# A recomputed hand-written order for a fused attention and gated-FFN kernel

## The chip, the cores and the metric

The kernel runs on one core of a Trainium2 chip. The metric is the device time of one execution in microseconds; before the change it is 292.96 us (median of 3 runs, 292.79 to 294.41). The profiled execution took 292.72 us, of which 290.2 us lie between its first and its last instruction. Times of instructions below are counted from that first instruction.

## The reference

```
B, H, S, Nb, D = 8, 8, 576, 16, 64
k_all, v_all = concat([beacon_k, k]), concat([beacon_v, v])     # 16 + 576 keys
scores = q @ k_all.T / sqrt(D), causal over the last 576 keys, beacons always seen
x = softmax(scores) @ v_all           # rearranged to [B*S, H*D] = [4608, 512]
out = ((x @ w1) * (x @ w2)) @ w3 @ w_out    # w1, w2: 512 x 1024; w3: 1024 x 1024; w_out: 1024 x 512
```

Inputs and output are float32; the kernel computes with float16 operands and float32 sums.

## The kernel before, in words

Everything is held on the chip. `w3 @ w_out` is folded once into `Wt` (1024 x 512), so that a block of 512 rows of `x` needs the two projections (`a`, `b`), a product and one output matmul. There are 8 batches of attention and 9 blocks of 512 rows (`mc`), and TensorE works on both kinds of work in turn.

What sets the order of the work is a string, `ORDER`, with some 1,190 entries. The loop in line 665 calls a small function for each entry, and each engine gets its instructions in exactly this order; an instruction whose operand isn't ready blocks all that stand behind it on its engine. The entries, with batch `b`, 128-row chunk `c`, PSUM bank `n` and evicting engine (`A` for ScalarE, ACT; `D` for VectorE, DVE):

- Loads. `lq b c`, `lk b c`, `lv b c` load a chunk of q, k or v (for batch 0, a pair of heads of q or k), `lkb`, `lvb` the beacons, `l3 r` a block of 128 rows of w3 (line 398), `lo a` two blocks of w_out (line 401), `l1 c`, `l2 c` a 256-column block of w1 or w2 (line 389). All are issued by GpSimd (POOL) on one software queue, in order, and a load waits for the landing of the one that had its semaphore before, eight loads earlier. Only `lq 0 0` and `lk 0 0` are issued by SyncE and ScalarE on queues of their own; these are the two first queues of the change's name.
- Folding. `t3 r n` transposes a w3 block on TensorE (line 481), `e3` evicts it, `f r a n` multiplies it by a quarter of w_out (line 491), four of them make a row block of `Wt`, and `ew` evicts that.
- Attention. `cast` and `tq`, `tk` (TensorE transposes) with `eq`, `ek` (evictions) bring q and k into place for batches 0 to 2; later batches (and `Dq 2 4`) use DMA transposes on SyncE (`Dq`, `Dk`). `s b g n` computes a group of score blocks (line 504; 13 groups `g` a batch, the two heads of a pair as matmuls on 64 rows each), `exp` is the activation on ACT (line 517), `m` masks the diagonal on DVE, `v b t h n` is the product with v (line 533) and `n` normalizes it on DVE (line 547; a reciprocal and a multiplication).
- `x` with `ex` transposes a chunk of the result on TensorE, `TX` by DMA instead (line 573). `a mc kf n` and `b mc kf n` are the projections (line 578; `a` with w1, `b` with w2, four matmuls of 512 columns), `ea` evicts the first to SBUF with a factor (ACT or DVE), `eb` multiplies the second by it (DVE only). `o mc mt n` is the output matmul (line 601), `eo` its eviction, `st` the store.
- `spin reps n` multiplies zeros (line 619) where TensorE would be idle at the start. `consts` are memsets and mask selections.

PSUM has one pair of banks for scores always (0), two pairs that are scores or single banks by turns (2 and 4), and two single banks (6, 7). There are three buffers for `ea` results (`asb`) and two of the transposed q, k, v and x. The casts of batch 0's q and k, `ea`, `eo`, `eq`, `ek`, `ex`, `e3` and `ew` name their engine in `ORDER`.

Of the kernel before, what the change touches and what calls it, by code (L numbers as in the profile page):

```python
# [190 lines left out]
def kernel(  # L191
# [427 lines left out]
    def spin(reps, n):  # L619
        for _ in range(reps):  # L620
            nc.tensor.matmul(bank(n), zeros[:, 0:P], zeros)
# [76 lines left out]
```

## Time and profile before

| engine | busy us of 290.2 | what it mostly does |
|---|---|---|
| TensorE, matmuls (PE) | 282.4 | projections, output, scores, PV, folding |
| ACT | 163.9 | 104 exp of 128 x 1024, evictions |
| DVE | 154.2 | `eb`, masks, normalizing, evictions |
| POOL | 133.5 | issues 26.19 MB of transfers on the software queue |

| load | us from issue to landing, median |
|---|---|
| w3 block | 6.1 |
| w_out blocks | 7.1 |
| w1, w2 block | 7.5 |
| 128-row chunk of q, k, v | 6.7 to 7.3 |
| first q, k on the SyncE and ACT queues | 4.2, 4.5 |

How to read this. The view of groups gives the busy time and the mean of one instruction of each kind; the view of waits gives, for each engine, whom it waited for. The landing of one load is its issue time in the timeline plus the time to landing that the DMA view gives for a stretch with this issue alone. Matmuls are pipelined, so the mean duration of one (379 ns for 512 columns) isn't its cost; the step from one start to the next is. The mean clock granted to TensorE was 1.000.

### The profile page before, as it was taken

How to read it: one execution, taken by the hardware profiler on the slowest of the kernel's cores; microseconds unless marked ns; L12 is line 12 of the kernel's file. 1: busy time of each engine (PE TensorE's matmuls, PEld its weight loads, DVE VectorE, ACT ScalarE, POOL GpSimd, SP SyncE). 2: the span in 40 equal slices, each digit the busy share in tenths (PEclk: the TensorE clock that was granted, in tenths of full speed). 3: DMA queues.
4: the chain of work that ended last, by engine and by line, in shares of the span. 5: the costliest groups of instructions: out<-in, count | busy, mean ns of one | idle time of the engine just before them, and what ended most of it. 6: DMA issues, size and time to landing. Idle time of an engine off the chain costs nothing.

```text
span 290.2 us, 7029 instructions
## 1 busy us (share of the span) xinstructions
PE 282.4 (97%) x2904; PEld 154.3 (53%) x2904; DVE 154.2 (53%) x344; ACT 163.9 (56%) x214; POOL 133.5 (46%) x186
## 2 busy tenths in 40 slices
PE   6999989999999999999999999999999999999995
PEld 2556655566565565565455544555465544444443
DVE  4338754786567677655456625534555653144500
ACT  3469655868684875386375527844475653232232
POOL 8579878996985452950956602930011001000000
PEclk9999999999999999999999999999999999999999
DMA  7999999999999999999999993999324014100033
GB/s 169 202 196 170 190 173 172 155 141 166 169 180 136 138 153 192 126 143 199 148 169 182 167 169 80 129 148 220 45 93 111 0 29 126 73 2 0 0 146 145
DMA packets 154319, 38.84 MB, mean 134 GB/s; under 512 B 144048, under 2 KB 149936, under 8 KB 154288
## 3 DMA queue, kind: packets, MB, share of 16 engines
q0 software_dynamic: 114720, 26.19, 99.2%
q1 hardware_dynamic: 39360, 11.92, 27.3%
q8 instruction: 22, 0.36, 0.5%
q10 hardware_dynamic: 208, 0.29, 0.3%
q14 instruction: 9, 0.07, 0.1%
HBM read 39.32 MB, written 9.44 MB: 168 GB/s over the span
## 4 chain that ended last, share of the span: by engine, by line
PE 84%; DMA 8%; POOL 5%; ACT 1%; issue 1%; DVE 0%; POOLq 0%
PE one L580 44%; PE one L601 21%; PE one L539 9%; PE pair L508 8%; DMA wo<-in_moe_w_out_dram 5%; DMA q<-in_q_dram 3%; PE one L428 1%; POOL va L340 1%; PE one L565 1%; POOL w L390 1%; POOL xT L399 1%; ACT ring L518 1%; POOL q L332 1%; POOL k L340 1%; POOL st L357 0%
## 5 line engine op out<-in xcount | busy, mean ns | idle before, releaser
L580 PE MATMUL one<-xT,w 128*128 128x512 f16 x576 | 133.0, 379 | 0.2 <-DVE xT L296 0.2
L518 ACT ACTIVATE ring<-pair 128x1024 f16<-128x1024 f32 x104 | 99.2, 1027 | 15.1 <-PE pair L508 14.8
L580 PEld LDWEIGHTS <-w 128*128 128x128 f16 x576 | 53.2, 98 | 59.9 <-issue 2.5
L595 DVE TENSOR_TENSOR gT<-one,asb 128x512 f16<-128x512 f32 x72 | 49.4, 690 | 55.1 <-PE one L580 41.3
L601 PE MATMUL one<-Wt,gT 128*128 128x512 f16 (+1 forms) x296 | 66.3, 373 | 0.0
L300 ACT ACTIVATE asb<-one 128x512 f32<-128x512 f32 x55 | 32.9, 599 | 58.7 <-PE one L580 37.1
L615 POOL DMA_DIRECT2D out_dram<-st x26 | 14.8, 569 | 69.9 <-DVE st L302 26.3
L601 PEld LDWEIGHTS <-gT 128*128 128x128 f16 x296 | 27.8, 98 | 30.2 <-issue 0.5
L340 POOL DMA_DIRECT2D va<-in_v_dram x40 | 34.0, 856 | 19.7 <-PE one L539 14.2
L539 PEld LDWEIGHTS <-ring 128*128 128x128 f16 x960 | 34.8, 97 | 10.2 <-issue 2.0
L539 PE MATMUL one<-va,ring 128*128 128x65 f16 x960 | 37.7, 193 | 0.5 <-DMA va<-in_v_dram 0.5
L300 ACT ACTIVATE st<-one 128x512 f32<-128x512 f32 (+1 forms) x26 | 15.1, 582 | 34.4 <-PE one L601 34.4
L551 DVE TENSOR_TENSOR x<-one,rd 128x384 f16<-128x384 f32 (+1 forms) x64 | 31.4, 491 | 2.2
L340 POOL DMA_DIRECT2D k<-in_k_dram x35 | 29.9, 860 | 4.5 <-issue 1.6
L332 POOL DMA_DIRECT2D q<-in_q_dram x35 | 30.2, 869 | 1.9 <-DMA q<-in_q_dram 0.9
L508 PE MATMUL pair<-qT,kT 64*128 64x80 f16 (+4 forms) x736 | 30.1, 225 | 0.1
L508 PEld LDWEIGHTS <-kT 64*128 64x128 f16 x736 | 19.9, 95 | 14.0 <-issue 10.2
L528 DVE TENSOR_TENSOR ring<-ring,MD 128x768 f16<-128x768 f16 x32 | 17.7, 553 | 10.2 <-ACT ring L518 10.2
L550 DVE RECIPROCAL rd<-one 128x6 f32<-128x6 f32 (+1 forms) x64 | 11.8, 185 | 20.7 <-PE one L539 20.5
L528 DVE TENSOR_TENSOR ring<-ring,MX 128x384 f16<-128x384 f16 x32 | 11.3, 352 | 10.1 <-ACT ring L518 9.9
L493 PE MATMUL one<-wo,gT 128*128 128x512 f16 x56 | 14.9, 380 | 0.4 <-DVE gT L296 0.3
L302 DVE TENSOR_SCALAR asb<-one 128x512 f32<-128x512 f32 x17 | 11.7, 689 | 3.5 <-PE one L580 3.5
(60 smaller groups left out, 126.8 us busy)
## 6 DMA issues: line engine op xcount, KB each, us to landing
out_dram<-st POOLq DMA_DIRECT2D x26, 256.0 KB, 6.2
...
```

What stands on the lines that cost most here:

```text
L300: nc.scalar.activation(dst, src, AF.Copy, scale=by)
L332: nc.gpsimd.dma_start(dst[:rows, c], src[b, :, ds(c * P, rows), :].rearrange("h s d -> s h d"))
L340: nc.gpsimd.dma_start(dst[ds(p0, rows), c], src[b, :, ds(s0, rows), :].rearrange("h s d -> s h d"))
L493: nc.tensor.matmul(bank(n), wT(r)[:, a, rt % 2, :], wo16[:, rt, :], start=(rt == 0), stop=(rt == NFT - 1),)
L508: nc.tensor.matmul(shape(n, "pair")[:, hh, ds(col, w)], kT[ds(hh * 64, 64), t, ts(jt, P)], qT[ds(hh * 64, 64), t, ds(q0, w)],)
L518: nc.scalar.activation(held(b, g)[:, :, 0:GW], shape(n, "pair"), AF.Exp, scale=scale)
L528: nc.vector.tensor_tensor(blk, blk, msk, ALU.mult)
L539: nc.tensor.matmul(pv[:, 2 * at + hh, 0 : D + 1], held(b, g)[:, hh, ds(col, P)], va[:, jt, 2 * t + hh, 0 : D + 1], start=(jt == 0), stop=( ...
L551: nc.vector.tensor_tensor(x16s[b % NB2][:, ds(2 * h, ni), ts(t, P)].rearrange("p i (h d) -> p i h d", h=2), pv[:, 0 : 2 * ni, 0:D].rearran ...
L580: nc.tensor.matmul(bank(n), w12[:, kt, ds(i * DF + kf * P, P)], xT[:, kt, ds(mc * 512, 512)], start=(kt == 0), stop=(kt == NKT - 1),)
L595: nc.vector.tensor_tensor(gTs[mc % 2][:, kf, :], bank(n), asb[slot["asb", (mc, kf)]], ALU.mult)
L601: nc.tensor.matmul(bank(n)[:, 0:w], gTs[mc % 2][:, kf, ts(mt, P)], Wt[:, kf, ds(c0, w)], start=(kf == 0), stop=(kf == NFT - 1),)
```

## The change

It gives a new `ORDER`, from the first entry to the last, recomputed for the landings of the two first queues, with the evicting engines (`A` or `D`) chosen by the same search. Loads of k and of the beacons now stand between the first w3 and w_out blocks. `TX 4 4` becomes `x 4 4 6` with `ex 4 4 D 6`. The last block to be finished is block 8, row tile 2, in place of block 7, row tile 0. Counts of engines, before and after: `ea` 55 A, 17 D and 33 A, 39 D; `eo` 26 A, 11 D and 15 A, 22 D; `e3` 8 D and 5 A, 3 D; `cast` 6 A, 2 D and 2 A, 6 D; `eq` 4 A, 9 D and 7 A, 6 D. The functions are as before but for one, which lets a spin write to the score pair:

```
 def spin(reps, n):
     for _ in range(reps):
-        nc.tensor.matmul(bank(n), zeros[:, 0:P], zeros)
+        nc.tensor.matmul(bank(n) if n else tiles[0][:, 0, :], zeros[:, 0:P], zeros)
```

The two orders up to the scores of batch 2 (the rest, some 85 lines on either side, is left out):

```
-consts 0; lq 0 0 S; lk 0 0 A; l3 2; consts 1; spin 8 7; l3 4; l3 3; lo 0; lkb 0 P; cast 0 0 q A;
-lo 1; l3 0; consts 2; spin 1 7; tq 0 0 6; cast 0 0 k A; l3 1; eq 0 0 D 6; spin 3 7; tk 0 0 7;
-ek 0 0 A 7; spin 2 6; t3 2 6; lq 0 1 P; e3 2 D 6; spin 2 7; t3 4 7; lkb 1; e3 4 D 7; spin 2 6;
-t3 3 5; lo 2; e3 3 D 5; spin 2 7; f 4 0 6; lk 0 1 P; tn 0 7; f 2 0 5; lk 1 0 P; en 0 A 7; s 0 0 0;
-s 0 1 2; lo 3; exp 0 0 0; f 2 1 5; f 4 1 6; f 3 0 7; exp 0 1 2; m 0 0 0; lv 0 4; s 0 2 0; f 3 1 7;
-exp 0 2 0; m 0 0 1; t3 0 4; lk 0 2 P; t3 1 3; e3 0 D 4; cast 0 1 q A; lk 0 3 P; e3 1 D 3; f 0 0 2;
-lq 0 2 P; tq 0 1 4; f 0 1 2; eq 0 1 A 4; l3 6; f 4 2 6; f 2 2 5; cast 0 1 k A; lvb 0; f 1 0 4;
-l3 5; tk 1 0 3; f 1 1 4; ek 1 0 A 3; f 1 2 4; tk 0 1 3; lq 0 3 P; f 2 3 5; ek 0 1 A 3; lq 1 1 P;
-f 3 2 7; ew 2 D 5; f 3 3 7; cast 0 2 k A; lkb 2; f 1 3 4; ew 3 D 7; f 4 3 6; lv 0 1; cast 0 3 k A;
-tk 0 2 5; ew 1 D 4; f 0 2 2; lv 0 0; ek 0 2 A 5; cast 0 2 q D; tk 0 3 7; ew 4 D 6; tq 0 2 4;
-ek 0 3 A 7; f 0 3 2; lk 1 4 P; eq 0 2 D 4; t3 6 6; ew 0 A 2; lv 0 3; s 0 3 0; s 0 4 4; s 0 5 2;
-e3 6 D 6; exp 0 3 0; lvb 1; f 6 0 7; t3 5 6; cast 0 3 q D; lv 0 2; exp 0 5 2; m 0 1 0; f 6 1 7;
-e3 5 D 6; f 6 2 7; l1 3; exp 0 4 4; s 0 6 0; s 0 7 2; m 0 1 1; l3 7; tq 0 3 6; exp 0 7 2; f 6 3 7;
-lq 1 0 P; eq 0 3 D 6; f 5 0 5; l2 1; f 5 1 5; ew 6 D 7; exp 0 6 0; tk 1 4 6; f 5 2 5; l1 1;
-ek 1 4 D 6; f 5 3 5; m 0 2 0; tq 1 1 6; l1 0; ew 5 A 5; eq 1 1 D 6; v 0 1 0 7; lq 1 3 P; v 0 0 1 5;
-n 0 1 0 7; v 0 0 0 6; n 0 0 1 5; l2 0; s 0 8 2; s 0 9 0; s 0 10 4; n 0 0 0 6; lq 1 4 P; exp 0 8 2;
-v 0 2 0 7; lk 1 3 P; t3 7 6; n 0 2 0 7; exp 0 10 4; v 0 1 1 3; lk 1 1 P; e3 7 D 6; tq 1 0 7;
-exp 0 9 0; s 0 11 4; n 0 1 1 3; f 7 0 6; lq 1 2 P; f 7 1 6; m 0 2 1; exp 0 11 4; s 0 12 2;
-eq 1 0 D 7; f 7 2 6; m 0 3 0; exp 0 12 2; v 0 2 1 7; l1 2; m 0 3 1; f 7 3 6; n 0 2 1 7; v 0 3 1 5;
-ew 7 A 6; lk 1 2 P; v 0 3 0 4; n 0 3 1 5; tq 1 3 6; l2 3; n 0 3 0 4; x 0 1 7; eq 1 3 A 6; x 0 2 5;
-x 0 3 3; ex 0 1 D 7; ex 0 2 A 5; x 0 4 6; x 0 0 4; lv 1 4; ex 0 3 D 3; ex 0 4 A 6; ex 0 0 D 4;
-tq 1 4 7; l2 2; eq 1 4 A 7; a 0 3 5; lv 1 0; b 0 0 6; ea 0 3 A 5; lv 1 2; b 0 3 7; lv 1 3; a 0 1 5;
-eb 0 3 7; tk 1 1 4; lq 2 0 P; ea 0 1 A 5; tk 1 3 7; ek 1 1 D 4; tq 1 2 3; b 0 1 2; ek 1 3 A 7;
-lv 1 1; eq 1 2 D 3; tk 1 2 7; eb 0 1 2; a 0 0 5; ek 1 2 A 7; lk 2 0 P; a 0 2 7; ea 0 0 A 5;
-lk 2 2 P; eb 0 0 6; s 1 0 0; s 1 1 2; s 1 2 4; ea 0 2 A 7; lq 2 2 P; exp 1 1 2; b 0 2 6; lq 2 1 P;
-a 0 4 7; exp 1 2 4; m 1 0 1; lq 2 4 P; eb 0 2 6; b 0 4 3; exp 1 0 0; lk 2 1 P; ea 0 4 D 7; a 0 6 6;
-eb 0 4 3; lk 2 3 P; s 1 3 4; s 1 4 0; s 1 5 2; m 1 0 0; ea 0 6 A 6; lq 2 3 P; exp 1 3 4; tq 2 0 7;
-v 1 0 0 6; eq 2 0 D 7; lv 2 0; n 1 0 0 6; tk 2 0 7; exp 1 5 2; a 0 5 5; lk 2 4 P; ek 2 0 D 7;
-m 1 1 0; exp 1 4 0; lk 3 2 P; tk 2 2 6; b 0 5 7; m 1 1 1; ek 2 2 D 6; lk 3 0 P; ea 0 5 A 5;
-s 1 6 2; s 1 7 0; s 1 8 4; eb 0 5 7; exp 1 6 2; lv 2 1; Dq 2 4; v 1 1 0 6; tq 2 2 7; n 1 1 0 6;
-lq 3 4 P; exp 1 8 4; tq 2 1 3; v 1 0 1 2; lv 2 3; eq 2 2 D 7; tk 2 1 6; eq 2 1 D 3; exp 1 7 0;
-tk 2 3 7; lk 3 3 P; b 0 7 5; ek 2 1 D 6; ek 2 3 D 7; lkb 3; v 1 1 1 6; n 1 0 1 2; tq 2 3 7;
-a 0 7 4; lv 2 4; n 1 1 1 6; eq 2 3 A 7; m 1 2 1; tk 2 4 7; lv 2 2; b 0 6 6; ea 0 7 A 4; ek 2 4 D 7;
-m 1 2 0; lq 3 3 P; s 1 9 0; s 1 10 2; eb 0 7 5; exp 1 9 0; v 1 2 0 7; lvb 2; eb 0 6 6; o 0 1 5;
-lk 3 1 P; n 1 2 0 7; exp 1 10 2; lq 4 1 P; m 1 3 0; v 1 2 1 7; eo 0 1 A 5; lq 3 1 P; s 1 11 0;
-s 1 12 2; s 2 0 4; n 1 2 1 7; exp 1 11 0; st 0 1 P; Dk 3 2; v 1 3 0 6; lq 4 3 P; o 0 0 7;
-n 1 3 0 6; exp 2 0 4; Dk 3 0; m 1 3 1; exp 1 12 2; m 2 0 0; s 2 1 0; s 2 2 4; s 2 3 2; eo 0 0 D 7;
...
+consts 0; lq 0 0 S; lk 0 0 A; l3 3; consts 1; spin 8 7; lk 0 1 P; lkb 0 P; lk 1 4 P; lkb 1; lo 0;
+cast 0 0 q A; cast 0 0 k D; lq 0 1 P; consts 2; spin 2 7; tq 0 0 6; l3 1; tk 0 0 7; eq 0 0 A 6;
+ek 0 0 D 7; spin 1 0; t3 3 5; lo 1; e3 3 A 5; lo 2; spin 1 6; tn 0 6; spin 1 7; tk 1 4 7; l3 4;
+cast 0 1 k A; ek 1 4 D 7; lo 3; en 0 A 6; spin 3 5; tk 0 1 4; lq 0 3 P; s 0 0 0; s 0 1 2;
+ek 0 1 A 4; lk 1 0 P; f 3 0 7; cast 0 1 q D; exp 0 0 0; tq 0 1 6; l3 0; s 0 2 4; exp 0 1 2;
+m 0 0 0; l3 5; eq 0 1 A 6; t3 1 3; m 0 0 1; l3 2; f 3 1 7; exp 0 2 4; e3 1 D 3; s 0 3 0; s 0 4 2;
+s 0 5 4; lq 1 3 P; exp 0 3 0; f 3 2 7; f 1 0 6; exp 0 5 4; m 0 1 0; lv 0 1; f 1 1 6; f 1 2 6;
+exp 0 4 2; m 0 1 1; t3 4 5; lv 0 2; f 1 3 6; e3 4 D 5; f 3 3 7; ew 1 A 6; lvb 1; cast 0 3 q D;
+f 4 0 4; ew 3 A 7; tq 0 3 6; lk 0 3 P; tk 1 0 5; eq 0 3 A 6; f 4 1 4; ek 1 0 D 5; f 4 2 4; lvb 0;
+t3 0 6; f 4 3 4; e3 0 A 6; ew 4 D 4; t3 5 7; lk 0 2 P; f 0 0 5; e3 5 A 7; f 0 1 5; lq 0 2 P;
+t3 2 6; f 5 0 7; lq 1 4 P; e3 2 A 6; tq 1 3 4; f 5 1 7; eq 1 3 D 4; lv 0 3; f 5 2 7; f 5 3 7;
+lv 0 0; f 0 2 5; ew 5 A 7; f 0 3 5; lv 0 4; cast 0 3 k D; f 2 0 7; ew 0 A 5; f 2 1 7; lk 1 2 P;
+cast 0 2 k D; tk 0 3 6; tk 0 2 5; l1 0; ek 0 3 A 6; f 2 2 7; cast 0 2 q D; ek 0 2 D 5; tq 0 2 4;
+l3 7; tq 1 4 6; f 2 3 7; eq 0 2 A 4; l3 6; ew 2 D 7; eq 1 4 A 6; spin 1 5; s 0 6 0; s 0 7 2; l1 3;
+exp 0 6 0; lq 1 2 P; spin 1 5; v 0 0 1 6; exp 0 7 2; m 0 2 0; v 0 0 0 7; l1 1; n 0 0 1 6; s 0 8 4;
+s 0 9 0; s 0 10 2; exp 0 8 4; l2 1; n 0 0 0 7; v 0 1 0 6; lq 1 0 P; tk 1 2 7; n 0 1 0 6; exp 0 9 0;
+v 0 2 0 5; v 0 1 1 4; m 0 2 1; lq 1 1 P; t3 7 6; ek 1 2 A 7; m 0 3 0; n 0 1 1 4; lk 1 1 P;
+s 0 11 0; exp 0 10 2; v 0 3 0 7; n 0 2 0 5; t3 6 4; lk 1 3 P; exp 0 11 0; v 0 2 1 3; n 0 3 0 7;
+e3 6 D 4; l2 0; x 0 0 5; e3 7 A 6; x 0 4 7; s 0 12 0; ex 0 4 D 7; f 6 0 4; lv 1 0; ex 0 0 D 5;
+exp 0 12 0; f 7 0 7; m 0 3 1; f 6 1 4; n 0 2 1 3; v 0 3 1 6; l2 3; f 6 2 4; n 0 3 1 6; f 6 3 4;
+lv 1 2; tq 1 2 5; ew 6 D 4; x 0 2 6; eq 1 2 A 5; x 0 1 3; tq 1 0 2; lv 1 4; ex 0 2 D 6; x 0 3 4;
+ex 0 1 A 3; f 7 1 7; eq 1 0 D 2; l2 2; ex 0 3 A 4; tq 1 1 6; f 7 2 7; eq 1 1 D 6; a 0 0 5; l1 2;
+a 0 1 6; lv 1 3; ea 0 0 D 5; a 0 3 4; ea 0 1 D 6; lq 2 2 P; tk 1 1 5; ea 0 3 D 4; tk 1 3 6;
+ek 1 1 A 5; b 0 1 3; lq 2 0 P; ek 1 3 A 6; f 7 3 7; eb 0 1 3; b 0 2 6; lkb 2; ew 7 D 7; b 0 0 5;
+lq 2 4 P; lv 1 1; a 0 2 7; eb 0 0 5; s 1 0 0; s 1 1 2; s 1 2 4; ea 0 2 D 7; lk 2 3 P; exp 1 0 0;
+eb 0 2 6; b 0 3 7; exp 1 2 4; lk 2 2 P; m 1 0 0; a 0 4 6; eb 0 3 7; lv 2 0; exp 1 1 2; a 0 5 5;
+lq 2 3 P; a 0 6 7; ea 0 4 A 6; m 1 0 1; lk 2 1 P; ea 0 5 A 5; s 1 3 0; s 1 4 2; s 1 5 4;
+ea 0 6 D 7; exp 1 3 0; lq 2 1 P; tq 2 2 6; Dq 2 4; tq 2 0 7; eq 2 2 D 6; lk 2 0 P; exp 1 5 4;
+s 1 6 0; eq 2 0 D 7; v 1 0 0 6; m 1 1 0; b 0 6 7; lv 2 3; n 1 0 0 6; exp 1 6 0; m 1 1 1; tk 2 3 5;
+lk 2 4 P; v 1 1 0 6; exp 1 4 2; m 1 2 0; tk 2 2 4; lv 2 4; n 1 1 0 6; s 1 7 0; s 1 8 2; lq 3 1 P;
+ek 2 3 A 5; ek 2 2 D 4; v 1 2 0 6; eb 0 6 7; exp 1 7 0; lv 2 2; v 1 0 1 5; n 1 2 0 6; tq 2 3 7;
+b 0 4 4; lk 3 0 P; exp 1 8 2; n 1 0 1 5; tk 2 1 6; lq 3 4 P; eq 2 3 D 7; v 1 1 1 5; ek 2 1 A 6;
+lkb 3; eb 0 4 4; tq 2 1 7; tk 2 0 3; eq 2 1 A 7; n 1 1 1 5; b 0 5 6; lq 3 0 P; ek 2 0 A 3; m 1 2 1;
+lvb 2; s 1 9 0; s 1 10 4; s 1 11 2; eb 0 5 6; exp 1 9 0; lk 3 1 P; tk 2 4 7; a 0 7 6; ek 2 4 D 7;
+lq 3 3 P; exp 1 11 2; m 1 3 0; v 1 3 0 7; ea 0 7 D 6; lv 2 1; s 1 12 0; s 2 0 2; exp 1 10 4;
+m 1 3 1; Dq 3 1; b 0 7 6; lk 4 1 P; n 1 3 0 7; exp 1 12 0; v 1 2 1 5; lq 3 2 P; eb 0 7 6; Dk 3 0;
+x 1 4 7; exp 2 0 2; x 1 0 4; n 1 2 1 5; v 1 3 1 6; lk 3 3 P; s 2 1 0; s 2 2 2; Dq 3 0; ex 1 4 D 7;
+ex 1 0 A 4; lk 3 2 P; m 2 0 0; o 0 2 7; exp 2 1 0; n 1 3 1 6; lvb 3; Dq 3 4; lk 4 2 P; exp 2 2 2;
+m 2 0 1; s 2 3 4; s 2 4 0; s 2 5 2; eo 0 2 D 7; lk 3 4 P; Dq 3 3; exp 2 3 4; lq 4 3 P; v 2 0 0 6;
...
```

## The prediction

> **What bounds the kernel now.** I read the page's engine shares first, then TensorE's waits.
>
> ```profile
> PE 282.4 (97%) x2904; PEld 154.3 (53%) x2904; DVE 154.2 (53%) x344; ACT 163.9 (56%) x214; POOL 133.5 (46%) x186
> ```
>
> TensorE is busy for 282.4 of 290.2 us, so a reordering can only win what TensorE idles or spins away, and every added wait costs its full length. The view of waits, for TensorE alone:
>
> ```profile
> PE one L621 <- DVE zeros L625: 1.3, 1, 1.3
> PE one L422 <- ACT o16q L296: 1.0, 1, 1.0
> PE one L428 <- DMA q<-in_q_dram: 0.5, 1, 0.5
> PE one L539 <- DMA va<-in_v_dram: 0.5, 1, 0.5
> ```
>
> They lie in the first 42 us, as the table by stretch says (columns: stretch, length, then busy us of PE, PEld, DVE, ACT and POOL, clock, DMA share, GB/s):
>
> ```profile
> 6.00:12.00 6.00, 6.00 (x73) 3.70 (x72) 2.83 (x4) 1.43 (x3) 4.10 (x8) 1.00 1.13 203
> 12.00:24.00 12.00, 11.55 (x106) 6.32 (x100) 5.62 (x10) 9.40 (x13) 9.08 (x14) 1.00 1.35 198
> 24.00:42.00 18.00, 16.64 (x282) 11.21 (x280) 13.44 (x35) 12.93 (x17) 15.14 (x20) 1.00 1.93 175
> 42.00:60.00 18.00, 17.85 (x206) 10.35 (x204) 10.33 (x23) 12.62 (x17) 16.89 (x22) 1.00 2.20 165
> 120.00:240.00 120.00, 120.00 (x1202) 63.63 (x1201) 63.55 (x138) 68.62 (x87) 43.01 (x59) 1.00 1.21 127
> ```
>
> After 60 us TensorE has no wait worth a name. Before that the DMA share is above 1 all along: the start is a race against loads. The chain of waits in 30 to 42 us shows which load ends it:
>
> ```profile
> 31.03 8.44 DMA q<-in_q_dram
> 39.48 0.05 issue
> 39.52 0.40 PE one L428 x4
> ...
> 41.67 0.38 PE one L580
> ```
>
> The load is `lq 1 3`; two places later `lq 1 4` lands (issued 32.65, 8.5 us to landing: 41.13), and the first `a` of the projections starts at 41.67. From there to the last matmul at 286.4 there are 244.7 us. Adding up the steps between matmul starts (216 ns for 512 columns, 56 for 128, 29 for 65), this is 242.7 us of work and 2.0 of waits: 0.6 behind batch 2's loads at 54 to 58 us, 1.4 in some 10 ns at each of many changes of operation.
>
> **What the Trainium skill says.** "TensorE: Matmul & The Clock Gate", Back-to-back issue gap, gives a warm gap of N/2.4 + 2.5 ns, 216 for 512 columns; the trace has 215 to 216, not the 131 that it also gives for sustained streams, and I use the trace. "DMA: Bandwidth & Descriptors", Issuing engines are not separate DMA queues: loads from all queues share the same 16 DMA engines. The trace agrees: the two loads on the SP and ACT queues land at 5.0 and 5.3, the first w3 block at 6.1, and then one lands after the other. "Perfetto Trace Analysis", What "DMA-bound" means, counts as a limit also an issuing engine whose track is solid with issues; here POOL is busy 16.89 of 18.00 us at 42 to 60.
>
> **The change, part by part.**
>
> *Work.* Counted from both orders, projections, output matmuls, score groups and PV blocks are the same. The zero matmuls (spins) go from 20 to 18: -0.43 us, but in the first 28 us, where loads decide, so I count 0. One DMA transpose (`TX 4 4`) becomes four TensorE transposes of 80 columns and an eviction: 4 x 35 ns = +0.14 on TensorE. The score matmuls stand in 41 separate runs in place of 39. Entering a run costs: the step into it is 311 ns where 216 is usual, and three groups take 774 ns where 1,536 columns are 640. That is 0.23 a run, +0.46.
>
> *Landings.* From the trace, one load after the other: w3 and w_out 1.23 us, w1 and w2 1.31, a head pair of batch 0 0.76, a 128-row chunk 0.84 to 0.87, chunk 4 of k 0.53 and of q 0.42, beacons 0.17. In the new order the last load of batch 1's q is `lq 1 1`, wanted before the first `a`. Up to it the same loads go as up to `lq 1 4` before, except that `lq 1 2` and `lk 1 2` (1.68) replace `l2 0` and `lkb 2` (1.48): 41.13 + 0.2 = 41.3.
>
> *POOL at the start.* An issue occupies POOL:
>
> ```profile
> 3.95 0.58 POOL L369 DMA_DIRECT2D b<-in_beacon_k_dram  x1
> 5.02 0.57 POOL L399 DMA_DIRECT2D xT<-in_moe_w_dram  x1
> 6.79 0.69 POOL L357 DMA_DIRECT2D st<-in_q_dram  x1
> ```
>
> So 0.6 us whether the load takes 1.2 us or 0.17. Before, seven of the first eight issues are big. Now four small ones stand early, and `l3 1` follows eight issues and four mask selections: 1.33 + 0.68 + 0.31 + 0.65 + 0.58 + 0.72 + 0.57 + 0.57 + 0.69 + 0.88 = 7.0. Issue to landing was never under 4.8 us for such a block, so it lands at 11.8, where data alone would say 11.0. The queue has run dry for 0.8 to 0.95 us, and everything after is later by that. Bounds for `lq 1 1`: 41.3 (a backlog makes it up) and 42.3. I take 42.0, as no slack follows until all of batch 1 is in.
>
> *Work behind that load.* Before, all w3 folding was done at the first `a`. Now `f 7 2` and `f 7 3` come later (+0.86), one transpose of k less (-0.22), with the 0.14 and the 0.46 above: 242.7 + 1.24 = 244.0. End of matmuls: 42.0 + 0.05 + 244.0 + 1.4 of small steps = 287.45, which is +1.05 against 286.4. Later loads give about the same: `lv 2 1`, now 35 loads and 27.2 us of the above durations behind `lq 1 1`, should land at 69.2 to 71.5 (POOL needs 0.88 for a chunk) and has 215.2 us of work behind it, with 1.3 of small steps 285.7 to 288.
>
> *Evictions.* ea goes from 55 on ACT and 17 on DVE to 33 and 39, eo from 26 and 11 to 15 and 22, five e3 go to ACT, four casts to DVE. One is
>
> ```profile
> L300 ACT ACTIVATE asb<-one 128x512 f32<-128x512 f32 x55 | 32.9, 599 | 58.7 <-PE one L580 37.1 <-DVE gT L595 20.6 <-ACT ring L518 0.9
> L302 DVE TENSOR_SCALAR asb<-one 128x512 f32<-128x512 f32 x17 | 11.7, 689 | 3.5 <-PE one L580 3.5
> L518 ACT ACTIVATE ring<-pair 128x1024 f16<-128x1024 f32 x104 | 99.2, 1027 | 15.1 <-PE pair L508 14.8
> ```
>
> 33 moved evictions take 20 us from ACT and give 23 to DVE (to 61% of the span); from 90 us on this lies under TensorE's work: 0. An e3 on ACT is not in the trace; 512 and 576 columns take 585 and 640 ns there, so 1,024 take about 1.03 (bounds 0.69, DVE's, and 1.17, two copies of 512). It stands in the load-bound start, where ACT then has about 13 us of work in the 12 after 6 us; up to 1 us late, hidden by later landings.
> What is not hidden: the order packs the softmax of batches 1 and 2. From `s 1 3` to `s 2 3` TensorE has 16.0 us of work. ACT has 13 exp, 4 copies of q and k and one of x: 15.9. DVE has 8 m (3.6), 8 n (5.9), 4 eb (2.8), 2 ea (1.4), 6 copies (2.5): 16.2. Before, the like stretch has 14.0, 13.9 and 16.4. ACT and DVE are released by each other there (exp, mask, PV, normalize), and the best 12 us of ACT before are 86% busy. At 90 to 95% such a stretch takes 17 to 18 us: +1 to +2, of which a part lies under waits for batch 2's loads; 0 to 2, I take 0.8. Behind a late exp, all later ACT evictions queue, and the score and PV matmuls wait for them.
>
> Sum: 1.05 + 0.8 = +1.85, or 294.8 us. The tail (last output in two halves) has the same form.
>
> **The rivals.**
> - *No difference.* The queue doesn't run dry: `lq 1 1` at 41.3, and packed exps hide: 41.35 + 244.0 + 1.4 = 286.75, +0.3, so 293.3. For it: 8 loads may be in flight, and the waits before had a backlog of 7 to 8 us to landing. Against it: POOL's 0.6 us for a beacon. Chance 0.28.
> - *Faster.* Loads after the first w3 blocks land sooner than their sum (the bubble of 0.6 us before `lv 0 3` and the 0.5 before `lk 1 0` don't recur, -1.1), and batch 2's waits of 0.6 vanish: 286.75 - 1.7 = 285.05, -1.35, so 291.6. For it: 2 us of waits between 12 and 42 that an order could save. Against it: the bytes ahead of the last q load are the same. Chance 0.20.
> - *Packed exps as the bound.* ACT at 86%, the best seen, from `s 1 0` to `s 2 11`, where it has 26.7 us of work and TensorE 28.0: 26.7 / 0.86 = 31.0, +3.0, and the late loads +1.05: 297.0. For it: the counts above. Against it: PSUM has two score pairs and the banks to lean on. Chance 0.15 of the 0.52 that I give to slower; the forecast itself 0.37.
>
> **How the numbers follow.** Forecast 294.8. The low end 292.4 takes in the no-difference case and part of the faster one, the high end 297.2 the packed case. Faster 0.20, same 0.28, slower 0.52: the forecast is only 0.4 us above the limit of 294.4.
>
> **What would show it.** Right: `lq 1 1` lands at 41.5 to 42.3 and a transpose of q waits for it; `l3 1` lands at 11.5 or later; ACT or DVE over 90% busy between 53 and 71 us, with score or PV matmuls waiting for them. Wrong: all of batch 1's q in by 41, or TensorE idle under 0.2 us in that stretch; or waits after 100 us, where I put none.

## The result, and the profile after

| kernel | median us | lowest to highest | runs |
|---|---|---|---|
| before | 293.19 | 291.93 to 295.03 | 6 |
| changed | 296.88 | 295.37 to 298.44 | 6 |

The ratio is 1.0119, 95% interval 1.0070 to 1.0169: the changed order is slower by 3.7 us (2.1 to 5.0). The forecast of 294.8 us has the sign and half the size. The ratios of this document leave out three executions in a slower state of the chip, two of the last experiment and one of the kernel before. The profiled execution took 296.59 us, with a span of 294.7 us where it was 290.2.

First the page of the changed kernel, its row of engines:

```profile
PE 286.0 (97%) x2906; PEld 155.6 (53%) x2906; DVE 172.5 (59%) x371; ACT 148.5 (50%) x188; POOL 133.6 (45%) x186
```

TensorE is again busy for 97%, and the row hides what happened. The work of the two orders is the same (below), yet 3.6 us more is called busy: the ends of the matmul records are modelled, so part of the waiting is inside them. The view of waits of TensorE (engine, line, whom it waited for: us in total, times, longest) shows what is new:

```profile
PE one L621 <- DVE zeros L625: 1.3, 1, 1.3
PE one L484 <- DMA xT<-in_moe_w_dram: 1.3, 2, 1.1
PE one L422 <- ACT o16q L296: 0.6, 1, 0.6
PE one L422 <- DVE o16q L296: 0.5, 1, 0.5
PE one L428 <- DMA k<-in_k_dram: 0.4, 1, 0.4
PE pair L508 <- DMA qT<-q: 0.4, 1, 0.4
PE one L493 <- DMA wo<-in_moe_w_out_dram: 0.3, 1, 0.3
```

In the kernel before, one load of q and one of v stood in this list. Now there are w3 (line 484), w_out (line 493) and k (line 428), and a new kind of entry: the scores wait for a transposed q (line 508). The table by stretch of the changed kernel (columns as in the prediction):

```profile
6.00:12.00 6.00, 5.71 (x60) 3.73 (x60) 1.51 (x3) 3.43 (x7) 4.55 (x11) 1.00 1.24 154
12.00:24.00 12.00, 10.65 (x104) 5.68 (x103) 5.39 (x10) 9.57 (x12) 7.27 (x11) 1.00 1.42 194
24.00:42.00 18.00, 16.43 (x261) 10.89 (x260) 10.12 (x28) 12.18 (x16) 14.90 (x20) 1.00 1.57 163
...
120.00:240.00 120.00, 120.00 (x1261) 64.46 (x1255) 72.01 (x155) 65.85 (x81) 42.48 (x58) 1.00 1.20 130
```

The last column is to be read against 203, 198 and 175 GB/s before. From 6 to 12 us the transfers lost 49 GB/s, which is 0.29 MB; from 12 to 24, 0.05; from 24 to 42, 0.22. Together 0.56 MB, at 194 GB/s 2.9 us of transfers. In the second profile of each kernel (from the repeats below) the rates are 201, 198 and 170 before and 175, 192 and 171 after, together 0.21 MB or 1.1 us: the loss from 6 to 12 us comes again, the one from 24 to 42 us does not. Nothing was added to be loaded; the same bytes came later. After 120 us TensorE is busy throughout, as before.

Because busy time says little here, I use a measure of my own from the trace, the **lost time** of TensorE: the start of an instruction less the time of all work ahead of it in its order, counted with the prediction's steps (216 ns for 512 columns, 56 for 128, 29 for 65, 0.23 us for entering a run of scores). By these steps alone the sums of work are 276.5 us before and 276.6 after. The table allows about 4 us more in both orders for the start, where the zero matmuls step at 427 ns. How much is allowed there moves a row as a whole, and with it the differences between the kernels, by 0.2 us; the growth from one column to the next it leaves alone. Apart from that, a difference in lost time is waiting. There are two profiles of each kernel, the second ones from the repeats below:

| lost time in us, up to | 12 | 20 | 30 | 44 | 70 | 100 | 124 | end |
|---|---|---|---|---|---|---|---|---|
| before | 0.36 | 1.27 | 1.42 | 3.89 | 4.39 | 4.95 | 5.13 | 5.99 |
| before, repeated | 0.48 | 1.81 | 1.98 | 4.22 | 4.71 | 5.29 | 6.41 | 7.26 |
| changed | 2.46 | 4.26 | 5.34 | 8.17 | 8.86 | 9.35 | 10.21 | 11.01 |
| changed, repeated | 1.22 | 3.38 | 4.32 | 6.57 | 7.33 | 8.36 | 10.02 | 10.83 |
| mean difference | 1.42 | 2.28 | 3.13 | 3.31 | 3.55 | 3.74 | 4.35 | 4.30 |

So about 3.3 of the 4.3 us are lost by 44 us, most of it already by 30, before the last load of batch 1's q; 0.4 from 44 to 100; 0.6 from 100 to 124; nothing after that. 4.3 (4.1 by the bare steps) is the mean of two differences of profiled executions that are far apart, 5.0 and 3.6; the timed medians differ by 3.7, and the interval holds the mean.

POOL's timeline at the start of the changed kernel (start us, length us, what; in brackets the idle time before, and its releaser):

```profile
6.04 0.72 POOL L648 TENSOR_SCALAR_AFFINE_SELECT MX<-MX 128x112 f16<-128x112 f16 x2
6.72 0.28 POOL L648 TENSOR_SCALAR_AFFINE_SELECT MD<-MD 128x128 f16<-128x128 f16 x1
6.96 0.57 POOL L399 DMA_DIRECT2D xT<-in_moe_w_dram  x1
...
11.78 0.86 POOL L340 DMA_DIRECT2D k<-in_k_dram  x1 [1.45 <-DMA wo<-in_moe_w_out_dram]
```

The third line is `l3 1`. It is issued at 6.96, and lands at 13.48. Before the issue at 11.78 POOL stands still for 1.45 us, because the load issued eight before has not landed: the queue that was all but empty at 6 us (the four small loads landed 3.6 to 4.7 us after their issue) is now full of blocks that come late.

The chain of waits between 98 and 121 us of the changed kernel (start us, length us, what) shows the end of the last wait:

```profile
112.52 0.64 SPq L477
...
113.25 6.54 DMA qT<-q
119.79 0.04 issue
119.84 0.57 PE pair L508 x16
```

This is `Dq 4 4`, the DMA transpose of the last chunk of batch 4's q, and `s 4 0 2` waits for it: its blocks of 80 columns are the ones that need this chunk. (The expectations below name `s 4 1 4`, the entry right behind it.) It is the last of four transposes in a row on SyncE, of which the first, `Dk 4 0`, was issued at 108.67, when `lk 4 0` had just landed (108.61). POOL had issued that load at 101.75. In the kernel before, `lk 4 0` was issued at 77.35 and `Dq 4 4` landed at 110.33.

The moved evictions are there, at the durations that the prediction used (groups of the changed kernel, busy us and mean ns of one):

```profile
L300 ACT ACTIVATE asb<-one 128x512 f32<-128x512 f32 x33 | 19.7, 601 | 69.8 <-PE one L580 53.6
L302 DVE TENSOR_SCALAR asb<-one 128x512 f32<-128x512 f32 x39 | 26.8, 690 | 11.3 <-PE one L580 10.8
```

### The profile page after: what moved, and what is told of

The parts are those of the page before. It is cut to its first block, busy times and chain, and to the rows that moved or that the text cites. A ratio compares the mean times of both kernels' runs of the same rounds, so it can differ in the third digit from the quotient of the medians.

```text
span 294.7 us, 7049 instructions
## 1 busy us (share of the span) xinstructions
PE 286.0 (97%) x2906; PEld 155.6 (53%) x2906; DVE 172.5 (59%) x371; ACT 148.5 (50%) x188; POOL 133.6 (45%) x186
## 4 chain that ended last, share of the span: by engine, by line
PE 80%; DMA 13%; POOL 3%; issue 1%; ACT 1%; DVE 1%; SPq 0%; POOLq 0%; ACTq 0%
PE one L580 41%; PE one L601 20%; PE one L539 8%; PE pair L508 7%; DMA xT<-in_moe_w_dram 3%; DMA q<-in_q_dram 3%; DMA wo<-in_moe_w_out_dram 2%; DMA qT<-q 2%; DMA k<-in_k_dram 2%; ACT ring L518 1%; PE one L428 1%; PE one L565 1%; POOL va L340 1%; POOL st L357 1%; PE one L493 0%
## 5 line engine op out<-in xcount | busy, mean ns | idle before, releaser
L580 PE MATMUL one<-xT,w 128*128 128x512 f16 x576 | 132.9, 379 | 0.0
L580 PEld LDWEIGHTS <-w 128*128 128x128 f16 x576 | 53.2, 98 | 58.9 <-issue 1.8
L300 ACT ACTIVATE asb<-one 128x512 f32<-128x512 f32 x33 | 19.7, 601 | 69.8 <-PE one L580 53.6
L601 PEld LDWEIGHTS <-gT 128*128 128x128 f16 x296 | 27.7, 98 | 30.5 <-issue 0.9
L539 PEld LDWEIGHTS <-ring 128*128 128x128 f16 x960 | 36.0, 97 | 12.2 <-issue 1.7
L539 PE MATMUL one<-va,ring 128*128 128x65 f16 x960 | 39.3, 193 | 0.1
L302 DVE TENSOR_SCALAR asb<-one 128x512 f32<-128x512 f32 x39 | 26.8, 690 | 11.3 <-PE one L580 10.8
L508 PE MATMUL pair<-qT,kT 64*128 64x80 f16 (+4 forms) x736 | 30.8, 225 | 0.6 <-DMA qT<-q 0.4
L302 DVE TENSOR_SCALAR st<-one 128x512 f32<-128x512 f32 x22 | 15.2, 691 | 17.6 <-PE one L601 17.6
L550 DVE RECIPROCAL rd<-one 128x6 f32<-128x6 f32 (+1 forms) x64 | 11.8, 184 | 12.7 <-PE one L539 12.1
L300 ACT ACTIVATE st<-one 128x512 f32<-128x512 f32 (+1 forms) x15 | 8.6, 574 | 20.0 <-PE one L601 20.0
```

The lines of the kernel that those rows point to most:

```text
L300: nc.scalar.activation(dst, src, AF.Copy, scale=by)
L302: nc.vector.tensor_scalar(dst, src, by, None, ALU.mult)
L508: nc.tensor.matmul(shape(n, "pair")[:, hh, ds(col, w)], kT[ds(hh * 64, 64), t, ts(jt, P)], qT[ds(hh * 64, 64), t, ds(q0, w)],)
L539: nc.tensor.matmul(pv[:, 2 * at + hh, 0 : D + 1], held(b, g)[:, hh, ds(col, P)], va[:, jt, 2 * t + hh, 0 : D + 1], start=(jt == 0), stop=( ...
L580: nc.tensor.matmul(bank(n), w12[:, kt, ds(i * DF + kf * P, P)], xT[:, kt, ds(mc * 512, 512)], start=(kt == 0), stop=(kt == NKT - 1),)
L601: nc.tensor.matmul(bank(n)[:, 0:w], gTs[mc % 2][:, kf, ts(mt, P)], Wt[:, kf, ds(c0, w)], start=(kf == 0), stop=(kf == NFT - 1),)
```

## The experiments

The theory after this reading: the loads set the start, the new order gives POOL small loads in runs, so bytes come later; the same happens to batch 2's v and batch 4's q and k. The rivals: the evicting engines, the packed softmax, or the order of the work on TensorE in itself. All times below were taken beside runs of the kernel before, whose medians were 293.20, 293.11 and 292.95 us in the three groups of runs. Diffs show only the entries of `ORDER` that move.

### Both kernels once more

No edit. The changed kernel:

> The changed kernel, unaltered, profiled once more. In its first profile the landings jump twice: the first w_out block (lo 0) lands 2.4 us later than its own 1.2 us explain, with 13 of its 16 engine completions at 8.4 to 9.2 us and three at 10.1, 11.4 and 11.5; and lk 1 2 lands 2.0 us late with one completion at 34.3 us. Theory 'the order of the loads does it': both jumps come back within 0.5 us at the same loads, lq 1 1 lands at 44.6, time about 3.5 us over before. Rival 'stalls of single DMA engines in one execution': the jumps are gone or elsewhere, lq 1 1 lands anywhere from 41.5 to 44.5, and the times of the rounds scatter by more than 1 us.

Measured: 296.90 us, ratio 1.0112 (1.0072 to 1.0151). TensorE's waits in this profile (line numbers are three lower in this file):

```profile
PE pair L505 <- DMA qT<-q: 1.2, 1, 1.2
PE one L481 <- DVE x L548: 1.0, 1, 1.0
PE one L481 <- ACT ring L515: 0.9, 1, 0.9
```

The time comes again, the places do so only in part. The two w_out blocks of `lo 0` landed at 9.39 in place of 11.49, `l3 1` at 12.41 in place of 13.48, `lq 1 1` at 43.00 in place of 44.57. The wait at `s 4 0 2` was longer instead (1.2 for 0.4), and ended at 119.65, where it had ended at 119.84. What had been gained at the start was lost again, 0.6 us of it at `v 2 0 0`, which waits for `lv 2 1`, and most of the rest at the transposes of batch 4: a deadline that POOL's issues set swallows what is won ahead of it.

The kernel before:

> The kernel before once more, unchanged, with a second profile: how far the landings of one kernel move from one execution to the next. If the start of the first profile (lq 1 3 at 39.48, lq 1 4 at 41.13, first a at 41.67) is typical, these come again within 0.5 us; if single slow transfers move them as in the two profiles of the changed kernel (lq 1 1 at 44.57 and 43.00), they differ by 1 us or more.

Measured: 292.82 us, ratio 0.9988 (0.9963 to 1.0012), span 291.4. Its start came again: `lq 1 3` at 39.81 (39.48 before), `lq 1 4` at 41.50 (41.13), first `a` at 42.00 (41.67), each within 0.4. But the timeline of TensorE from 108 to 118 us has

```profile
113.84 0.58 PE L508 MATMUL pair<-qT,kT 64*128 64x80 f16 x16 [0.77 <-DMA qT<-q]
```

`s 4 0 2` waits here too, since `Dq 4 4` landed at 113.80 and not at 110.33. In the first profile that landing was 2.25 us ahead of its use (112.58), and nothing in the waits told that the transposes of batch 4 are close to the edge. The changed order goes over it in both of its profiles; the order before did in one of two.

### The evicting engines, alone and undone

First the order of before with the `ea` and `eo` engines of the changed kernel:

```
-ea 0 3 A 5; ... ea 0 1 A 5; ...       (order of before, engines of before)
+ea 0 3 D 5; ... ea 0 1 D 5; ...       (order of before, engines of the changed kernel)
```

> The order of before, with the evicting engines of ea and eo as the changed kernel has them (39 ea and 22 row tiles of eo on DVE, in place of 17 and 11). Theory 'the engines are off the path': within 0.4 us of before, TensorE without new waits. Rival 'DVE becomes late': 1 to 2 us slower, with TensorE waiting for DVE's evictions between 40 and 130 us.

Measured: 295.63 us, ratio 1.0070 (1.0049 to 1.0092). So moving these evictions alone costs 2.1 us in the old order, where I had counted 0. TensorE's lost time grows by 1.81 from 70 to 124 us (0.74 and 1.70 in the two profiles of before) and by 1.72 after it (0.86 and 0.85). One wait of 0.3 us stands behind it in the list: `s 2 4 0` waits for an exp (`PE pair L504 <- ACT ring L514: 0.3, 1, 0.3`), which the kernel before doesn't have. The rest is spread over many steps, and I can't name it by line.

That asked for the other half: the changed order with the `ea` and `eo` engines of before (57 of 109 evictions change).

```
-ea 0 0 D 5; ... ea 0 1 D 6; ...       (changed order, its engines)
+ea 0 0 A 5; ... ea 0 1 A 6; ...       (changed order, engines of before)
```

> The changed order with the engines of the kernel before for the ea and eo evictions (57 of them change engine; f, e3, cast and all else as in the changed kernel). With the old order, the new engines alone cost about 2 us. Theory A, the engine choice is fitted to its order by the search, and either choice is wrong in the other's order: slower than the changed kernel, about 298.5 us. Theory B, more evictions on VectorE cost TensorE time in any order: about 294.9 us, 2 less than the changed kernel, with less growth of TensorE's lost time after 120 us. Theory C, the landings set the time in the new order and the engines do nothing there: 296.9, within 0.5.

Measured: 297.95 us, ratio 1.0169 (1.0130 to 1.0208). The same on the order with all loads regrouped (below):

> The changed order with all loads regrouped (as in the run all_loads, 294.87 us) and also with the evictions' engines of the kernel before. Theory A (fitted to the order): 296 to 297. Theory B (a loss everywhere): 292.9, level with the kernel before. Theory C (no matter here): 294.9.

Measured: 295.18 us, ratio 1.0093 (1.0056 to 1.0129), where that order has 1.0049 (1.0030 to 1.0068) with its own engines. In its profile, of an execution that took 297.18 us, the longest of its six, one wait in particular is new, at `a 3 2` (timeline of TensorE):

```profile
136.57 1.67 PE L577 MATMUL one<-xT,w 128*128 128x512 f16 x7 [1.05 <-DVE xT L293]
```

Theory B (a loss in any order) falls: putting the old engines back made neither order faster. In both the medians are higher (by 1.0 and 0.3 us; by the ratios, 1.7 and 1.3), as theory A has it, but the intervals overlap, so A and C (no matter) are not told apart. Firm is this: the new engines of `ea` and `eo` are a loss of 2.1 us in the old order, and in the new one no loss by them is seen, so they don't explain the 3.7 us. That they belong to their order fits both, but isn't shown. The engines of `cast`, `e3`, `eq` and the other evictions changed too, and no run puts those back.

### The old start with the new rest

The order of before up to `s 1 0 0`, then the changed one, with a few entries put right at the seam:

```
 consts 0; lq 0 0 S; lk 0 0 A; l3 2; ... lk 2 2 P; eb 0 0 6;      (order of before)
-s 1 0 0; s 1 1 2; s 1 2 4; ...                                   (rest of before)
+lq 2 2 P; lq 2 4 P; s 1 0 0; s 1 1 2; s 1 2 4; ...               (rest of the changed order)
```

Entries of the rest that the start had already done are left out, and `b 0 2` stands where the start had done `b 0 3`.

> The order of before up to the scores of batch 1 (s 1 0), the changed order from there on, with b 0 2 and b 0 3 exchanged and lq 2 2, lq 2 4 loaded first, so that the same work is done. Theory 'the first 44 us lose it': within 1 us of before, since 4.3 of the 5.0 us between the two profiles' sums of TensorE waits arise before s 1 0. Rival 'the packed softmax of batches 1 and 2 loses it too': 1.5 us or more over before, with ACT and DVE both over 90% busy for some 12 us after s 1 3.

Measured: 295.45 us, ratio 1.0081 (1.0059 to 1.0104). The lost time at 44 us is 3.87, that of before, and nothing is lost at `s 4 0 2`. But 1.46 are lost at `tq 2 2`, for which `lq 2 2` lands too late, and 0.54 at `b 0 2`, which waits for an eviction on DVE: both right behind the seam, and as large as what was to be seen. Another 0.5 at `v 2 0 0`, where `lv 2 1` lands at 72.63, is like the changed kernel's own. The run says that the old start is restored by the old entries, and no more; it doesn't measure the rest.

### The small loads between the first w3 blocks

One small pair later, with the transpose that uses it:

```
-... lk 0 1 P; lkb 0 P; lk 1 4 P; lkb 1; lo 0; ... tk 1 4 7; ... lo 3; ...
+... lk 0 1 P; lkb 0 P; lo 0; ... lo 3; lk 1 4 P; lkb 1; ... ew 3 A 7; tk 1 4 7; ek 1 4 D 7; ...
```

> The changed order, but lk 1 4 and lkb 1 stand behind lo 3 in place of behind lkb 0, and their transposes and evictions behind ew 3. Theory 'small loads between the first big ones let the queue run dry': lo 0 lands by 9.5 (11.5 in the changed kernel), l3 1 by 12, and if nothing else is lost lq 1 1 lands 1 to 2 us earlier, -1 to -2 us against the changed kernel. Rival 'the jump has nothing to do with small loads': lo 0 jumps as before or not at all independent of this, time within 0.5 us of the changed kernel.

Measured: 295.81 us, ratio 1.0093 (1.0058 to 1.0128). `lo 0` lands at 8.28 and `l3 1` at 10.26 (11.49 and 9.39, 13.48 and 12.41 in the changed kernel). The lost time at 12 us is 0.93. It is 3.07 at 20 us, 6.15 at 44 and 10.48 at the end: the first blocks are there, but `lq 1 1` lands at 42.53, `lv 2 1` at 73.39 and `Dq 4 4` at 119.26, and the scores of batch 4 wait for that as in the changed kernel. At 34 us another block, `l3 7`, comes too late: `t3 7 6` waits 0.86 us for it (1.10 in the first profile of the changed kernel; in the second, 1.02 for it and for DVE, which freed the bank as it landed, at 35.14). The median is 1.1 us lower than the changed kernel's, with overlapping intervals.

The reverse, the same four small loads put between the first w3 blocks of the order of before:

```
-l3 2; consts 1; spin 8 7; l3 4; l3 3; lo 0; lkb 0 P; ... lkb 1; ... lk 0 1 P; ... lk 1 4 P
+l3 2; consts 1; lk 0 1 P; lkb 0 P; lk 1 4 P; lkb 1; spin 8 7; l3 4; l3 3; lo 0; ...
```

> The order of before; only lk 0 1, lkb 0, lk 1 4 and lkb 1 are issued right behind the first w3 block, as in the changed order. Theory 'small loads among the first big ones cost the stream': 0.25 to 0.3 MB less moved by 12 us (before 2.19), the first a 1.0 to 1.5 us later than 41.7, 1.0 to 1.6 us slower than before. Rival 'their place is free': bytes within 0.05 MB, time within 0.5 us.

Measured: 293.75 us, ratio 1.0011 (0.9981 to 1.0040), span 291.6. In its profile the table by stretch has 177 GB/s from 6 to 12 us (203 and 201 before), `l3 1` lands at 16.61 (14.20 and 14.35 before), and the first `a` starts at 43.12 (41.67 and 42.00), 1.1 to 1.5 us later; the prediction's step says 0.8 to 0.95. By 12 us 2.01 MB have moved (2.19 and 2.15 before), a loss of half of what was expected. The last matmul starts at 287.83, where it was 286.38 and 287.66: against the second profile of before, nearly all of the delay is gone again by the end. In the timed runs the ratio makes it 0.3 us, and 1.2 at the upper end of the interval: in the old order this edit is worth a third of the loss of 3.7 us at the end of its interval, and perhaps nothing.

### The other runs of small loads, and all together

With the first edit kept, the run of small loads from `lvb 1` to `lv 0 4` gets big blocks between:

```
-... lvb 0; ... lq 1 4 P; ... l1 0; l3 7; ...
+... lvb 0; l3 7; ... lq 1 4 P; l1 0; ...
```

> small_late, and in the second run of small loads (lvb 1 to lv 0 4) two big ones: l3 7 behind lvb 0 and l1 0 behind lq 1 4. Theory 'a run of small loads starves the queue': bytes moved by 44 us rise from 7.81 MB in small_late to 7.95 MB or more (before: 8.06, changed kernel 7.44 and 7.68), TensorE's lost time up to 44 us falls from 6.2 to about 5.4 us. Theory 'batch 4's transposes set the end': the group s 4 1 4 still starts at 119.5 to 120, and the time is within 0.5 us of small_late. Rival 'the start sets the end': 0.8 us faster than small_late.

Measured: 295.40 us, ratio 1.0061 (1.0040 to 1.0082). `lq 1 1` lands at 41.90, but `lv 2 1` still at 73.50 and `Dq 4 4` at 119.29. The lost time at 44 us was to fall from 6.2 to 5.4; it is 6.92. The wait for `l3 7` is gone, but `lk 0 2` now stands behind that block, lands at 27.61 (26.34 without this edit), and `tk 0 2` waits 1.25 us for its cast. Alone, the loads of batch 4 further ahead:

```
-... lv 4 2; ... lq 5 1 P; ... lq 6 3 P; ... lk 4 0 P; ... lq 4 0 P; ... lk 4 4 P; ... lq 4 4 P
+... lv 3 0; lk 4 0 P; lq 4 0 P; lk 4 4 P; lq 4 4 P; ...
```

> The changed order; only lk 4 0, lq 4 0, lk 4 4 and lq 4 4 are loaded ahead of lv 4 2, lq 5 1, lq 6 3 and lk 5 2. Theory 'the landing of batch 4's last transposes sets the end': Dq 4 4 lands 2.5 to 3.5 us earlier than 119.8, the wait before s 4 1 4 (0.6 and 1.4 us in the two profiles) is gone, 0.6 to 1.4 us faster than the changed kernel. Rival 'the DMA engines are full there and it only moves the wait': another wait of like size at v 3 or v 4 takes its place, within 0.4 us of the changed kernel.

Measured: 296.18 us, ratio 1.0105 (1.0074 to 1.0137). The wait at `s 4 0 2` is gone (`Dq 4 4` lands at 116.42; lost time grows by 0.38 from 100 to 124 us, and by 0.86 and 1.66 in the changed kernel), but this profile has 10.01 lost at 100 us, and the time can't tell the 0.5 to 1.3 us. Both, with `lvb 2; lv 2 1` drawn ahead as well:

```
-... lv 2 2; ... lvb 2; ... lv 2 1; ...
+... lv 2 2; lvb 2; lv 2 1; ...
```

> The changed order with four regroupings of loads together: small_late, spread, batch4_early, and lvb 2 with lv 2 1 behind lv 2 2 (the first v 2 waited 0.3 to 1.2 us for lv 2 1). Theory 'the new order loses only by its loads': TensorE's lost time ends at 7 to 7.5 us (before 6.0, changed kernel 11.0 and 10.8), 294.2 to 294.8 us, that is 2 to 3 us faster than the changed kernel and about 1 us over before. Rival 'engines and packing lose too': less than 1.5 us faster than the changed kernel.

Measured: 294.87 us, ratio 1.0049 (1.0030 to 1.0068), below the interval of the repeat of the changed kernel. The table by stretch of this run has the old rate back from 6 to 12 us and from 24 to 42 us:

```profile
6.00:12.00 6.00, 4.87 (x66) 2.91 (x67) 1.47 (x3) 4.88 (x8) 5.00 (x9) 1.00 1.16 200
12.00:24.00 12.00, 11.48 (x111) 6.54 (x111) 5.45 (x10) 9.14 (x12) 7.86 (x12) 1.00 1.58 188
24.00:42.00 18.00, 15.97 (x258) 10.48 (x256) 11.39 (x30) 11.44 (x16) 16.37 (x21) 1.00 1.80 179
```

`lv 2 1` lands at 65.65, `Dq 4 4` at 111.91, and neither is waited for. The lost time at the end is 8.66, 2.3 less than the mean of the changed kernel; the medians say 2.0. So the grouping of loads is about 2 us of the 3.7. How the edits share it isn't measured: the medians fall from 296.90 to 295.81, 295.40 and 294.87, and each interval overlaps with the next. Nor is it mainly the start that gains. Against the repeat of the changed kernel the lost time at 44 us is only 0.1 lower (6.45 for 6.57), and at the end 2.2; against the first profile, whose start was the worse one, 1.7 and 2.4. `lq 1 1` lands at 41.10, as early as the prediction had it from data alone (41.3), and the first `a` still starts at 43.60, where the repeat has 43.72 with a landing at 43.00.

What remains, 1.8 us by the medians (lost time 8.66 against 5.99 and 7.26), lies between 12 and 44 us. The longest waits of this run there:

```profile
PE one L419 <- DVE o16k L293: 1.4, 1, 1.4
PE one L481 <- ACT ring L515: 0.9, 1, 0.9
```

The first is `tk 0 2` behind a cast that DVE now does. The timeline of DVE tells what the cast waited for:

```profile
27.61 0.63 DVE L293 COPY o16k<-st 96x768 f16<-96x768 f16 x1 [1.71 <-DMA st<-in_k_dram]
```

DVE had been idle for 1.71 us and started when `lk 0 2` had landed (27.59). So this wait comes from the load, and from the edit that put `l3 7` ahead of it, not from the engine: the bytes in sum are on time, this load isn't. The second is a transpose of w3 that waits for a PSUM bank which an exp of batch 0 must read first; it stands in both profiles of the changed kernel too (0.2 and 0.9). How much of the 1.8 us is the place of single loads, and how much the order of TensorE's work and its banks, no run here tells apart.

### A shorter start for the kernel before

```
-lq 1 1 P; ... lkb 2; ... lvb 1; ... l1 0; ... lq 1 3 P; ... lq 1 4 P; ... lq 1 2 P
+lq 1 1 P; ... lq 1 3 P; ... lq 1 4 P; l1 0; ... lq 1 2 P; lkb 2; lvb 1
```

> The kernel before with three loads that nobody wants soon put behind the loads of batch 1's q: l1 0 behind lq 1 4, lkb 2 and lvb 1 behind lq 1 2. If the landing of batch 1's q sets the start as the trace of before says, lq 1 3 lands about 1.3 us earlier, the first a of the projections starts at about 40.6 in place of 41.67, and the time falls by 0.8 to 1.2 us to 292.0 to 292.4. Rival: batch 2's loads at 54 to 58 us take the gain back, or the waits of the start lie elsewhere: within 0.5 us of 293.1.

Measured: 292.95 us, ratio 0.9999 (0.9973 to 1.0025): no gain to be seen, and 0.8 us at the end of the interval. `lq 1 3` lands at 37.33 (39.48) and `lq 1 4` at 39.77 (41.13), but the first `a` starts at 41.01 (41.67 and 42.00), 0.7 to 1.0 earlier and not 2.2. The timelines of DVE and TensorE in this run say what took the place of the load:

```profile
39.48 0.43 DVE L547 TENSOR_TENSOR x<-one,rd 128x256 f16<-128x256 f32 x1
39.82 1.04 DVE L292 COPY xT<-one 128x512 f16<-128x512 f16 x3
```

```profile
41.01 2.32 PE L576 MATMUL one<-xT,w 128*128 128x512 f16 x10 [0.36 <-DVE xT L292]
```

The first `a` needs all of batch 0's transposed `x`, and DVE, with the last normalization at 39.48 and three copies in a row behind it, has it ready at 40.86. So q and the attention of batch 0 end within a microsecond of each other, and taking one away uncovers the other. The row `PE one L580 <- DVE xT L296: 0.2` was in the waits of the kernel before, and I had passed over it. Then `tk 2 0` loses about 0.5 (0.3 before), starting at 54.41, just after `lk 2 0` lands (54.36; 53.93 before). What is left at the end, 5.68 of lost time for 5.99 and 7.26, the timed runs don't show. None of the runs beats the kernel before.

All runs together, as ratios to the kernel before:

| run | median us | ratio, 95% |
|---|---|---|
| changed, repeated | 296.90 | 1.0112 (1.0072 to 1.0151) |
| changed, one small pair later | 295.81 | 1.0093 (1.0058 to 1.0128) |
| ... and w blocks between | 295.40 | 1.0061 (1.0040 to 1.0082) |
| changed, batch 4 earlier alone | 296.18 | 1.0105 (1.0074 to 1.0137) |
| all loads regrouped | 294.87 | 1.0049 (1.0030 to 1.0068) |
| ... with the engines of before | 295.18 | 1.0093 (1.0056 to 1.0129) |
| changed, engines of before | 297.95 | 1.0169 (1.0130 to 1.0208) |
| before, new engines | 295.63 | 1.0070 (1.0049 to 1.0092) |
| before, then changed from `s 1 0` | 295.45 | 1.0081 (1.0059 to 1.0104) |
| before, small loads first | 293.75 | 1.0011 (0.9981 to 1.0040) |
| before, three loads later | 292.95 | 0.9999 (0.9973 to 1.0025) |
| before, repeated | 292.82 | 0.9988 (0.9963 to 1.0012) |

## Why the prediction was right or wrong

**The sum, +1.85.** Measured +3.7. The sign was right, and in part its reason: the bytes are the same, and loads that the order makes late cost time. The size was off in three terms and one was missing. That the forecast still came within 2.1 us is in part luck, for 0.8 of its 1.85 stood for a cause that was worth about 0.2.

**Work, +0.60.** The lost time after 124 us, where the score runs stand without loads, grows by 0.80 and 0.81 in place of 0.86 and 0.85. So the prices of the steps hold. The two spins less stand ahead of the landing from which the sum counts, so leaving them out of it was right.

**POOL at the start.** "Follows eight issues and four mask selections: ... = 7.0": `l3 1` was issued at 6.96 and 7.05. "Issue to landing was never under 4.8 us for such a block, so it lands at 11.8": it landed at 13.48 and 12.41, 6.5 and 5.4 us after its issue. I took the shortest landing of the trace for the price, and the mark that I set myself ("11.5 or later") was met by both while the number was low by 0.6 to 1.7. "The queue has run dry for 0.8 to 0.95 us": the missing 0.29 MB are 1.5 us at the rate of the next stretch, in the repeat (175 GB/s from 6 to 12 us) 0.9. The mechanism stood, and the reversed experiment showed it in the old order: 1.1 to 1.5 us at the first `a` of its profile, though hardly any of it in the timed runs.

**"Everything after is later by that", `lq 1 1` at 42.0.** It landed at 44.57 and 43.00, outside the bound of 42.3. Of the 2.6 and 1.0 us, 1.7 and 0.6 were there already at `l3 1`. The other 0.9 and 0.4 are a step that failed: I let the delay of the first 12 us run on unchanged, as if the stream behind it were that of before. The run with the small pair later shows that it isn't: there the first blocks land early (`l3 1` at 10.26), and `lq 1 1` still at 42.53, not at the 41.3 of data alone. In the changed kernel POOL issues without a pause from `lv 0 3` on, and the four loads from `lq 1 4` to `lv 0 4` land 4.0 to 4.5 us after their issue, where 6.7 to 7.3 is the median of a chunk: POOL, not the bytes, is the limit at the end of that run of small loads. With w blocks put between, the rate from 24 to 42 us rises from 167 to 179 GB/s and `lq 1 1` lands at 41.90. (The changed kernel has 163 and 171 GB/s there and the kernel before 175 and 170, which alone would not settle it.)

**That one landing as the path.** I counted all work behind `lq 1 1`, as though TensorE were on time until then. By 30 us, 13 to 15 us ahead of it, TensorE had already lost 5.34 and 4.32 us, where it had lost 1.42 and 1.98 before, to w3, w_out and casts. From 30 to 44 us the growth is 2.8 and 2.3, against 2.5 and 2.2 before. A transpose of q does wait, as I had named for a sign, but it is `tq 1 0` for `lq 1 0`, and it loses 0.35 and 0.33; `tq 1 1` comes 0.1 us after its load. So two paths, the loads of q and the folding ahead of them, end within 0.4 us of each other, and the landing alone decides little: with all loads regrouped it comes 1.9 us earlier than in the repeat, and the first `a` 0.1. That is why mending the first landings alone gave little.

**`lv 2 1` at 69.2 to 71.5.** 74.46 and 73.45: late with `lq 1 1`, and the 35 loads behind it took 29.9 and 30.5 us in place of 27.2. "POOL needs 0.88 for a chunk" was the right price, and I had used it for a bound only. In the table by stretch of the changed kernel, from 55 to 73 us:

```profile
55.00:73.00 18.00, 17.79 (x292) 11.76 (x291) 14.45 (x37) 16.01 (x21) 17.71 (x22) 1.00 2.22 144
```

POOL is busy for 17.71 of 18.00 us. The Trainium skill ("Perfetto Trace Analysis", What "DMA-bound" means) names just this, an issuing engine's track solid with issues, as a limit of its own. The trace agrees: 144 GB/s here and 140 in the repeat, 155 and 147 in the kernel before, where POOL is busy for 15.28 and 15.55 us of the same stretch. The issues of the 35 loads take 28.9 us together, more than the 27.2 that I had put for their landings.

**Packed softmax, +0.8.** Wrong in size. From `s 1 3` to `s 2 3` the changed kernel takes 16.68 us in both profiles, 0.7 over its 16.0 of work, of which about 0.5 is there in the order before too (lost time from 44 to 70 us: 0.69 and 0.76, against 0.50 and 0.49). So the term is about 0.2. Of the sign that I named, ACT or DVE over 90% busy from 53 to 71 us, ACT is at the edge (16.29 of 18.00 us, 90.5%, and 16.01 or 89% in the repeat), DVE at 80%:

```profile
53.00:71.00 18.00, 17.78 (x286) 11.67 (x282) 14.57 (x37) 16.29 (x21) 17.21 (x22) 1.00 2.28 144
```

And in its waits stands one more row:

```profile
PE pair L508 <- ACT ring L518: 0.2, 1, 0.2
```

This is a group of scores, `s 1 6 0`, that waits for an exp, 0.2 us in either profile. So the mechanism is there, and small. I took 86%, the best of before, for a ceiling; it was only what that stage asked for. The rival built on it (297.0) came near the time by a cause that it put at 3.0 us and that was worth 0.2.

**Evictions, 0.** For the change as a whole no run contradicts it. As a statement on moving evictions it was wrong: the same move of `ea` and `eo` in the old order costs 2.1 us. "This lies under TensorE's work" holds for the sum of ACT's and DVE's time, not for the moment at which a bank comes free.

**"Waits after 100 us, where I put none."** This was named as what would prove me wrong, and it did: `s 4 0 2` waits for `Dq 4 4`, 0.64 and 1.40 of lost time. Set against before (none in one profile, 0.94 in the other), about 0.6 us of the mean difference. I had read "no wait worth a name after 60 us" as slack; it was a landing 2.25 us ahead of its use, and I did not follow the loads of batch 4 through the new order: `lk 4 0` went from 77 to 102 us.

**The rivals.** "The queue doesn't run dry" falls with the 154 GB/s. "Faster" falls too: the bubbles did go elsewhere, but more came. What stays open is the cause of about 1.8 us of the loss, between 12 and 44 us, that stays when the loads are regrouped; part of it is a load that the regrouping itself made late.
